# Landmark sums on the vector engine from transposed q and k, PE transposes into bf16 PSUM, and the landmark softmax of the next batch ahead of the first layer of this one

## The chip, the cores and the metric

The kernel runs on one core of a Trainium2 chip. The metric is the device time of one execution in microseconds, as the median over several runs; lower is better. The engines are named as in the profile: PE (TensorE), DVE (VectorE), ACT (ScalarE), POOL (GpSimd) and SP (SyncE).

## The reference

The work is a Nyström attention followed by a two-layer block with a SiLU between the layers, both in float32. There are 8 batches, 8 heads, 576 positions of head size 64, and 32 landmarks, each the mean of 18 neighbouring positions. The second part has 4608 tokens, width 512 and hidden width 2048.

```python
q_lm = q.reshape(B, H, m, S // m, D).mean(axis=3)      # m = 32
k_lm = k.reshape(B, H, m, S // m, D).mean(axis=3)
A  = sm(q, k_lm);  Bm = sm(q_lm, k_lm);  C = sm(q_lm, k)   # sm: scaled softmax
Z = Bm.T / (norm1(Bm) * norminf(Bm) + 1e-6)
for _ in range(6):
    Z = 2 * Z - Z @ Bm @ Z
x = (A @ Z @ C @ v)            # tokens x 512 over the heads
h = x @ w_in;  g = h * sigmoid(h);  out = g @ w_out
```

## The kernel before

**A planner sets the order.** The kernel adds operations (`A(name, engines with planned costs, emit, dependencies, priority, ...)`) to a plan. `Plan.run` goes through simulated time, gives each free engine the ready operation of lowest priority number, and the program is emitted in that order. Every engine then runs its own queue strictly in that order on the chip: an instruction whose data is late holds up all that stand behind it on its engine.

**One batch** (`attn(b)`, `layer1(b)`, `layer2_batch(b)`). The eight heads of a batch sit in two groups g of four heads, on 128 partitions. The steps, with the names that the rest of this document uses:

- *Loads.* q, k and v come in through POOL's queue (L377, L384), weights too (L391 to L401). For batches from 2 on, `later_loads` gates the load of batch b on the transposes of batch b-2 (the buffer `qk` has two halves) and of batch b-1.
- *Transposes of q and k* into `qT`. Batches 0 and 1 (`NPE = 2`): on PE, each block as an ordinary product with the identity `idb` into f32 PSUM (L485), then a cast to bf16 on DVE or ACT (`copy`, L342 and L344). Batches 2 to 7: by DMA transposes on SP's queue (L506), four for a batch, which wait for the loads.
- *Landmark sums.* Batches 0 and 1 on PE (L524). Batches 2 to 7 on POOL: a tree of five kinds of f32 additions (`sa`, `sb`, `lm`, L543), ten instructions for a batch, straight from the loaded `qk`. `ltr` turns the sums on PE, `lmT` is the copy of that to SBUF.
- *Landmark softmax and its inverse.* `sb` (scores of landmarks, PE, L576), `pb` (exp, ACT, L588), row sums and `bm` (DVE, L595, L597), `bbd`, the norm, and then six Newton steps, each a PE product of `st` and a DVE instruction (L647). I call the steps from L595 to L647 the chain.
- *The wide softmaxes.* `C` and `A` (PE, L709 and L666), exp on ACT (`ce` L718, `et` L675), sums and their inverse by Ln and exp (L685, L689), `etn` on DVE (L694). C's probabilities are turned into `ct`: for batches below `NCT = 3` by PE products and casts, for the others by DMA transposes on SP (L744). `cv`, `wsb`, `zt` and `m` (L757 to L807) put the small matrices together with w_in.
- *First layer:* 16 wide PE products and 2 narrow ones for a batch, each followed by a SiLU on ACT (`gm` L838, `gx` L861).
- *Second layer:* seven half-size products for each pair of 128 tokens (Strassen's scheme), with four DVE sums of `gm` into `ss` (L927) ahead of them, and sums of w_out made once (`wt` and `w_out_sb`, L447, eight DVE instructions).

**ACT's two tables.** Exp and Ln share one table, SiLU has another, and a change of table costs an ACT_TABLE_LOAD. The planner therefore binds all exp work of a batch into a group (`group=f"x{b}"`), which opens only when no first layer is open and no SiLU may stand inside (L137 to L146). `pb` belongs to the group of its own batch, so the landmark softmax of batch b+1, and the chain behind it, begin when the first layer of batch b is through.

**Idle PE slots** below 45 us of the plan are filled with products of zeros (`zer`), whose results are not used.

Of the kernel before, what the change touches and what calls it, by code (L numbers as in the profile page):

```python
# [7 lines left out]
FP = mybir.dt.float32  # L8
# [10 lines left out]
class Op:  # L19


    def __init__(self, name, engs, emit, deps=(), prio=0.0, psum=0, cls=None, table=None,
# [6 lines left out]
        self.after = ()  # L29
        self.ins = None  # L30
# [14 lines left out]
class Plan:  # L45
# [16 lines left out]
    def run(self):  # L62
# [50 lines left out]
        while n < total:  # L113
# [7 lines left out]
            while moved:  # L121
                moved = False
                for e in ("PE", "ACT", "DVE", "POOL", "SP"):
# [3 lines left out]
                    for o in cand[e]:  # L127
# [11 lines left out]
                        if e == "ACT" and o.group is not None and group[0] != o.group:  # L139
                            if group[0] is not None:  # L140
                                continue
                            if l1_open:
                                continue
                            if len(l1_at) > 2:
# [38 lines left out]
                    switch = False  # L183
                    if e == "ACT" and o.table and o.table != table[0]:
                        dur += 1.3
                        table[0] = o.table
                        switch = True
                    if o.group is not None:
                        if group[0] is None:
                            group[0], group[1] = o.group, groups[o.group]  # L190
                            pending[0] = False
                        group[1] -= 1
# [66 lines left out]
def kernel(  # L259
# [26 lines left out]
    NCT = 3  # L286
# [21 lines left out]
    s1_r = ring(smp, [128, NG, JP, Dh], FP, "sa", 1)  # L308
    s2_r = ring(smp, [128, NG, 4, Dh], FP, "sb", 1)
# [5 lines left out]
    bbd_r = ring(smp, [128, NG, 4, L], BF, "bbd", 1)  # L315
    st_r = ring(smp, [128, NG, SW], BF, "st", 3)
# [34 lines left out]
    def either(n, act=True, dve=True):  # L351
# [5 lines left out]
        return r  # L357

# [93 lines left out]
    bones = hmask.rearrange("p a l -> p (a l)")  # L452


    last = {}
    tree = [None]
# [4 lines left out]
    def attn(b):  # L461
# [12 lines left out]
        if on_pe:  # L474
            blocks = {}
            me["qk_read"] = []
            for t in (1, 0):
                todo = [(g, jp) for g in range(NG) for jp in range(JP)]
                for i in range(0, 18, 4):
                    part = todo[i:i + 4]  # L480
# [11 lines left out]
                    def tcp(e, t=t, i=i, n=len(part), key=(t, i)):  # L492
                        copy(e, qT[:, t].rearrange("p g j x -> p (g j) x")[:, i:i + n, :],
                             bank(blocks[key])[:, 0:n * 128].rearrange("p (n x) -> p n x", x=128))
                    c = A(f"trc{t}{i}.{b}", either(128 * len(part)), tcp, [o], p0 + 8).reads(o)
# [22 lines left out]
        for t in (1, 0):  # L518
            if on_pe:
                for j0 in range(0, J, 6):  # L520
                    def lms(e, t=t, j0=j0):
                        ps = bank(me["lms", t])
                        for j in range(j0, j0 + 6):
                            mm(ps[:, 0:128], idb, qk[:, t, :, j, :], start=(j == 0),  # L524
                               stop=(j == J - 1))
                    o = A(f"lms{t}{j0}.{b}", [("PE", mm_us(128, 6))], lms,
# [551 lines left out]
```

## Time and profile before

| what | value |
|---|---|
| runs shown (3) | 275.11, 275.89, 276.56 us; median 275.89 us |
| the profiled execution | 276.69 us, of which the span from first to last instruction is 275.0 us |
| mean granted TensorE clock | 0.973 |
| busy: PE / ACT / DVE / POOL | 254.0 / 188.6 / 171.1 / 116.7 us |
| table loads on ACT | 13 x 1.283 us |
| moved by DMA | 37.29 MB |

The profile lists for each engine how long it was busy, for each group of like instructions their count, summed and mean duration and the idle time before them, and for an idle stretch the instruction whose end released it. The zero products count as PE busy. PEclk is the clock granted to PE in a stretch, 1.00 for full speed; a busy PE at a lower clock does less.

### The profile page before, as it was taken

The page shows a single profiled execution, that of the slowest core. Times are in us where ns is not written, and L with a number is a line of the kernel's source. Part 1 is how long each engine was busy: PE and PEld are TensorE (multiplying, and loading weights), DVE is VectorE, ACT ScalarE, POOL GpSimd, SP SyncE. Part 2 cuts the span into 40 slices and gives each one's busy share as a digit, 9 for nine tenths or more (in the row PEclk, how much of TensorE's full clock was granted, in tenths as well). Part 3 has the DMA queues.
Part 4 walks back from the last instruction along what each step waited for, and adds up shares of the span by engine and source line. Part 5 has one row for each costly group of instructions (what it writes and reads, how often), then busy time and mean ns, then how long its engine had stood idle before and what let it go on. Part 6 is the DMA issues. An engine that isn't in the chain of part 4 may idle for free.

```text
span 275.0 us, 7164 instructions
## 1 busy us (share of the span) xinstructions
PE 254.0 (92%) x2773; PEld 173.0 (63%) x2773; DVE 171.1 (62%) x381; ACT 188.6 (69%) x449; POOL 116.7 (42%) x133
## 2 busy tenths in 40 slices
PE   7999999859979979789997999999999999999993
PEld 5975545633657645446565556768777657588882
DVE  1477329964197784899389749616898739154621
ACT  1699997508976689857997875586756897852120
POOL 8337513997954964992598259700000000000000
PEclk9999999977979999979999999999999999999999
DMA  6999999999999899939975999913428300202433
GB/s 101 213 195 203 206 204 210 202 146 219 181 114 158 176 165 184 184 60 186 192 130 96 183 211 191 177 38 79 76 70 129 79 0 4 75 21 72 116 78 101
DMA packets 58593, 37.29 MB, mean 136 GB/s; under 512 B 39616, under 2 KB 49856, under 8 KB 58560
## 3 DMA queue, kind: packets, MB, share of 16 engines
q0 software_dynamic: 15232, 18.35, 40.3%
q1 hardware_dynamic: 43184, 18.30, 34.1%
q8 instruction: 21, 0.34, 0.5%
q10 hardware_dynamic: 144, 0.20, 0.2%
q14 instruction: 12, 0.10, 0.1%
HBM read 36.70 MB, written 9.44 MB: 168 GB/s over the span
## 4 chain that ended last, share of the span: by engine, by line
PE 63%; DVE 16%; DMA 8%; ACT 5%; issue 4%; POOL 2%; DVEq 0%; POOLq 0%; ACTq 0%
PE ps L332 63%; DMA w_in_sb<-in_moe_w_in_dram 8%; DVE ss L927 5%; ACT gm L838 3%; DVE m L344 3%; DVE gm L927 1%; DVE wt L447 1%; POOL qk L377 1%; DVE st L647 1%; DVE bm L597 1%; DVE ost L961 1%; DVE w_out_sb L447 1%; POOL v L384 1%; ACT m L342 1%; DVE etn L694 1%
## 5 line engine op out<-in xcount | busy, mean ns | idle before, releaser
L332 PE MATMUL ps<-etn,m 128*128 128x64 bf16 (+1 forms) x512 | 71.3, 289 | 0.2 <-DVE m L344 0.2
L838 ACT ACTIVATE gm<-ps 128x512 f16<-128x512 f32 x128 | 66.0, 635 | 3.1 <-PE ps L332 2.8
L332 PEld LDWEIGHTS <-gm 128*128 128x128 f16 x512 | 48.7, 99 | 15.1 <-issue 5.4
L332 PE MATMUL ps<-w_out_sb,gm 128*128 128x256 f16 (+1 forms) x392 | 54.7, 284 | 0.6 <-DVE w_out_sb L447 0.5
L342 ACT COPY ost<-ps 128x256 f32<-128x256 f32 (+1 forms) x59 | 21.9, 375 | 48.6 <-PE ps L332 47.2
L332 PEld LDWEIGHTS <-m 128*128 128x128 bf16 x512 | 32.3, 98 | 25.4 <-issue 3.3
L332 PEld LDWEIGHTS <-ss 128*128 128x128 f16 x408 | 38.8, 98 | 9.4 <-DVE ss L927 2.4
L543 POOL TENSOR_TENSOR sa<-qk 128x576 f32<-128x576 bf16 x24 | 33.0, 1394 | 15.4 <-DMA qk<-in_k_dram 14.9
L961 DVE TENSOR_TENSOR ost<-ost,ps 128x256 f32<-128x256 f32 x51 | 20.9, 416 | 28.7 <-PE ps L332 19.7
L332 PE MATMUL ps<-wt,ss 128*128 128x256 f16 x272 | 35.1, 277 | 1.2 <-DVE ss L927 1.2
L647 DVE SCALAR_TENSOR_TENSOR st<-st,ps 128x320 bf16<-128x320 bf16 (+3 forms) x54 | 21.5, 405 | 13.1 <-PE ps L332 12.6
L543 POOL TENSOR_TENSOR sb<-sa 128x512 f32<-128x512 f32 (+1 forms) x24 | 25.1, 1044 | 1.8
L344 DVE CAST m<-ps 128x512 bf16<-128x512 f32 x31 | 20.2, 682 | 3.5 <-PE ps L332 3.4
L342 ACT CAST m<-ps 128x512 bf16<-128x512 f32 x33 | 18.0, 589 | 4.7 <-PE ps L332 4.7
L927 DVE TENSOR_TENSOR ss<-gm 128x1024 f16<-128x1024 f16 x15 | 14.8, 999 | 8.5 <-ACT gm L838 8.5
L384 POOL DMA_DIRECT2D v<-in_v_dram x24 | 14.0, 591 | 11.4 <-DMA w_out_sb<-in_moe_w_out_dram 6.1
L332 PE MATMUL ps<-w_out_sb,ss 128*128 128x256 f16 x136 | 17.7, 273 | 0.5 <-DVE ss L927 0.4
L332 PE MATMUL ps<-st 128*128 128x160 bf16 (+1 forms) x96 | 14.7, 226 | 3.7 <-DVE st L647 2.8
L718 ACT ACTIVATE ce<-ps 128x288 bf16<-128x288 f32 x32 | 12.7, 410 | 6.4 <-PE ps L332 6.4
L332 PE MATMUL ps<-wt,gm 128*128 128x256 f16 x120 | 16.4, 282 | 0.4 <-DVE ost L961 0.4
L332 PE MATMUL ps<-w_in_sb,zt 64*32 64x512 bf16 x256 | 13.6, 412 | 3.2 <-DVE m L344 2.1
L344 DVE COPY ost<-ps 128x256 f32<-128x256 f32 (+1 forms) x11 | 4.9, 449 | 18.4 <-PE ps L332 17.7
(85 smaller groups left out, 367.2 us busy)
## 6 DMA issues: line engine op xcount, KB each, us to landing
out_dram<-ost SPq DMA_DIRECT2D x141, 64.0 KB, 1.7
qk<-in_k_dram POOLq DMA_DIRECT2D x8, 576.0 KB, 6.0
qk<-in_q_dram POOLq DMA_DIRECT2D x8, 576.0 KB, 8.7
v<-in_v_dram POOLq DMA_DIRECT2D x24, 192.0 KB, 10.3
w_out_sb<-in_moe_w_out_dram POOLq DMA_DIRECT2D x4, 512.0 KB, 10.5
w_in_sb<-in_moe_w_in_dram POOLq DMA_DIRECT2D x4, 256.0 KB, 9.2
w_in_sb<-in_moe_w_in_dram POOLq DMA_DIRECT2D x8, 128.0 KB, 7.0
qT<-qk SPq DMA_TRANSPOSE x24, 3.9
```

What stands on the lines that cost most here:

```text
L332: nc.tensor.matmul(out=out_ap, lhsT=lhsT, rhs=rhs, start=start, stop=stop, skip_group_check=True)
L342: nc.scalar.copy(out=out, in_=in_)
L344: nc.vector.tensor_copy(out=out, in_=in_)
L377: lambda e, t=t, src=src: nc.gpsimd.dma_start(out=qk_r[b % 2][:, t].rearrange("p g j d -> p g (j d)"), in_=src[b].rearrange("(g h) (l j) d ...
L384: lambda e, a=a: nc.gpsimd.dma_start(out=v_r[b % 2][a * L:(a + 1) * L, :, :], in_=v[b].rearrange("h (l a x) d -> a l h (x d)", l=L, a=VA)[ ...
L447: lambda e, o_=o_, x=x, y=y: nc.vector.tensor_tensor(out=o_, in0=x, in1=y, op=OP.subtract), dep, 400.0)
L543: lambda e: nc.gpsimd.tensor_tensor(out=o_, in0=a_, in1=b_, op=OP.add),
L647: nc.vector.scalar_tensor_tensor(out=s2[:, g0:g1, lo:SW], in0=s[:, g0:g1, lo:SW], scalar=2.0, in1=ps[:, 0:NG * SW].rearrange("p (g x) -> p ...
L718: nc.scalar.activation(out=ce[:, :, 0:VP].rearrange("p (i c) (a l) -> p c a i l", c=2, a=VA)[:, c], in_=bank(me[f"C{g}"], c)[:, 0:HS].rear ...
L838: lambda e, dc=dc, cell=cell: nc.scalar.activation(out=gm[:, dc, :], in_=bank(cell["o"]), func=AF.Silu),
L927: lambda e, o_=o_[:, k], x=x[:, k], y=y[:, k], op=op: nc.vector.tensor_tensor(out=o_, in0=x, in1=y, op=op), dep, 850.0 + prio / 100)
L961: nc.vector.tensor_tensor(out=out_, in0=x, in1=y, op=OP.add)
```

## The change

Five things change.

1. **Landmark sums of batches 2 to 7** move from POOL to DVE. They are made from the transposed `qT`, in f16, in four instructions for each of q and k (names `lra` to `lrd`, 1024, 512, 256 and 256 elements per partition; tiles `red` and `rs`). The ten POOL additions of a batch go. `ltr` becomes one PE product with a constant `fold` (f16), which also adds the last two halves.
2. **PE transposes** (q and k of batches 0 and 1, and `ct`) use the transpose instruction and write bf16 into PSUM. The copies of q and k are four for each of q and k instead of five, those of `ct` one for a group of heads instead of two. `NCT` goes from 3 to 4, so batch 3's `ct` goes over PE and no longer over SP.
3. **The landmark softmax of batch n+1** may now run while the exp table of batch n is still loaded: `sb` no longer waits for what the rest of its batch needs (`ready`), `pb` is marked `early`, and `A` and `C` carry `ready` and open the group instead. The SiLUs of batch 0 wait for `pb` of batch 1.
4. **Buffers:** `st` from 3 to 6 tiles and `bbd` from 1 to 2, so that two batches' chains may overlap.
5. **The order in which operations are added:** `attn(b)` before `layer1(b - 1)`.

How the planner's order moves is seen at two places. The first is ACT's queue around the first layer of batch 0. Before, from the last SiLU of batch 0 on (`gx`; `pb1` is the landmark softmax of batch 1, `ce` belongs to its wide softmax):

```order
L861 ACTIVATE gx_120<-ps4_74 128x8x64
L1036 ACT_TABLE_LOAD
L588 ACTIVATE pb1_93<-ps5_75 128x64
L718 ACTIVATE ce0_108,pbs1_95<-ps0_70 128x3x3x32
L718 ACTIVATE ce0_108,pbs1_95<-ps1_71 128x3x3x32
```

With the change, at the beginning of the same first layer (L358 is the copy, L620 `pb`, L874 the SiLU):

```order
L358 CAST m0_120<-ps6_76 128x512
L358 CAST lmT1_91<-ps5_75 128x256
L358 CAST m0_120<-ps0_70 128x512
L620 ACTIVATE pb1_93<-ps2_72 128x64
L874 ACT_TABLE_LOAD
L874 ACTIVATE gm0_122<-ps4_74 128x512
L358 CAST m0_120<-ps5_75 128x512
```

`pb1` has moved from behind the 18 SiLUs of batch 0 to ahead of them, and the table load of the SiLUs stands behind it.

The second place is DVE's queue behind the first layer of batch 0. Before (`wt` and `w_out_sb` are the sums of w_out, `st` the Newton steps of batch 1, `etn` and `wsb` its wide softmax):

```order
L447 TENSOR_TENSOR wt_121<-w_out_sb_79,wt_121 128x1024
L647 SCALAR_TENSOR_TENSOR st1_100<-st0_99,ps0_70 128x320
L447 TENSOR_TENSOR wt_121<-w_out_sb_79,wt_121 128x1024 x2
L647 SCALAR_TENSOR_TENSOR st2_101<-st1_100,ps0_70 128x320
L694 TENSOR_TENSOR etn1_107<-et0_102,ln0_104 128x576
L774 TENSOR_TENSOR wsb1_113<-ps4_74,pbs1_95 128x256
L694 TENSOR_TENSOR etn1_107<-et1_103,ln1_105 128x576
L647 SCALAR_TENSOR_TENSOR st0_99<-st2_101,ps0_70 128x320
L447 TENSOR_TENSOR wt_121<-w_out_sb_79,wt_121 128x1024
L447 TENSOR_TENSOR w_out_sb_79<-w_out_sb_79 128x4x256
```

With the change, the Newton steps of batch 1 (L680) stand in the first layer of batch 0:

```order
L662 TENSOR_TENSOR st3_103<-ps4_74,pbs1_95 128x2x128
L680 SCALAR_TENSOR_TENSOR st4_104<-st3_103,ps0_70 128x320
L680 SCALAR_TENSOR_TENSOR st5_105<-st4_104,ps0_70 128x320
L680 SCALAR_TENSOR_TENSOR st3_103<-st5_105,ps0_70 128x320
L468 TENSOR_TENSOR wt_125<-w_out_sb_79 128x1024
L680 SCALAR_TENSOR_TENSOR st4_104<-st3_103,ps0_70 128x320
L964 TENSOR_TENSOR ss0_126<-gm0_122 128x1024
```

and where the first layer of batch 1 begins (`m1` is its input), the landmark sums of batch 2 follow (L570, `red`):

```order
L360 CAST m1_121<-ps1_71 128x512
L468 TENSOR_TENSOR wt_125<-w_out_sb_79,wt_125 128x1024 x2
L468 TENSOR_TENSOR w_out_sb_79<-w_out_sb_79 128x4x256 x2
L570 TENSOR_TENSOR red_86<-qT0_82 128x1024
L998 TENSOR_TENSOR ost2_130<-ost2_130,ps5_75 128x256
L570 TENSOR_TENSOR red_86<-red_86 128x2x256
L998 TENSOR_TENSOR ost2_130<-ost2_130,ps6_76 128x256
```

The sums of w_out no longer stand between the Newton steps of batch 1, and DVE's queue now holds additions that wait for SP's transposes (`qT`), with outputs of the second layer (`ost`) behind them.

The diff, cut to its core:

```diff
@@ Plan.run
                         if e == "ACT" and o.group is not None and group[0] != o.group:
-                            if group[0] is not None:
+                            if o.early is not None and table[0] == "exp":
+                                pass
+                            elif group[0] is not None or l1_open:
                                 continue
-                            if l1_open:
+                            elif o.early is not None and any(
+                                    x.done is None or x.done > t + 1e-9 for x in o.early):
                                 continue
+                        if o.opens is not None and group[0] != o.opens and (
+                                group[0] is not None or l1_open or len(l1_at) > 2):
+                            if group[0] is None and not l1_open:
+                                pending[0] = True
+                            continue
...
-    NCT = 3
+    NCT = 4
-    s1_r = ring(smp, [128, NG, JP, Dh], FP, "sa", 1)
-    s2_r = ring(smp, [128, NG, 4, Dh], FP, "sb", 1)
+    red = smp.tile([128, NG, 4, 128], HF, tag="red", name="red")
+    rs = smp.tile([128, 2, NG, 128], HF, tag="rs", name="rs")
-    bbd_r = ring(smp, [128, NG, 4, L], BF, "bbd", 1)
-    st_r = ring(smp, [128, NG, SW], BF, "st", 3)
+    bbd_r = ring(smp, [128, NG, 4, L], BF, "bbd", 2)
+    st_r = ring(smp, [128, NG, SW], BF, "st", 6)
+    STEPS = (((0, 5), (5, 4), (9, 5), (14, 4)),) * 2
...
+    fold = constp.tile([128, 128], HF, tag="fold", name="fold")
+    def folds(e):
+        for r in (0, 64):
+            for c in (0, 64):
+                nc.vector.tensor_copy(out=fold[r:r + 64, c:c + 64], in_=idb[r:r + 64, r:r + 64])
...
-                        ps = bank(blocks[key])
+                        ps = bank(blocks[key]).bitcast(BF)
                         for n, (g, jp) in enumerate(part):
-                            mm(ps[:, n * 128:(n + 1) * 128],
-                               qk[:, t, g, 2 * jp:2 * jp + 2, :].rearrange("p j d -> p (j d)"),
-                               idb)
+                            nc.tensor.transpose(
+                                out=ps[:, n * 128:(n + 1) * 128],
+                                in_=qk[:, t, g, 2 * jp:2 * jp + 2, :].rearrange("p j d -> p (j d)"),
+                                identity=idb)
...
-                xs = [pool(f"la{g}", 576, s1[:, g], src[:, g, 0:9], src[:, g, 9:18],
-                           [qk_ops[b, t], tree[0]]) for g in range(NG)]
-                me["qk_read"] += xs
-                x = pool("lb", 512, s2, s1[:, :, 0:4], s1[:, :, 4:8], xs)
-                x = pool("lc", 256, s1[:, :, 0:2], s2[:, :, 0:2], s2[:, :, 2:4], [x])
-                x = pool("ld", 128, s2[:, :, 0], s1[:, :, 0], s1[:, :, 1], [x])
-                tree[0] = lm_ops[t] = pool("le", 256, lm[:, t], bc(s2[:, :, 0], 2, 2),
-                                           bc(s1[:, :, 8], 2, 2), [x] + prev2.get("ltrs", []))
+                src = qT[:, t]
+                x = lr("ra", 1024, red[:, :, 0:4], src[:, :, 0:4], src[:, :, 4:8],
+                       qt_ops[t, 0] + qt_ops[t, 1] + tree[0])
+                x = lr("rb", 512, red[:, :, 0:2], red[:, :, 0:2], red[:, :, 2:4], [x])
+                x = lr("rc", 256, red[:, :, 0], red[:, :, 0], red[:, :, 1], [x])
+                x = lr("rd", 256, rs[:, t], red[:, :, 0], src[:, :, 8], [x] + prev.get("ltrs", []))
...
+                if not on_pe:
+                    return mm(ps[:, 0:256], fold, rs[:, t].rearrange("p g x -> p (g x)"))
...
-        me["sb"] = A(f"sb.{b}", [("PE", 0.2)], sbm, lmT_all + ready, p0 + 11, psum=1,
+        me["sb"] = A(f"sb.{b}", [("PE", 0.2)], sbm, lmT_all + prev2.get("zt", []), p0 + 11, psum=1,
+        pb_op.early = ready
...
-                            lmT_all + [(pb_op, -0.2)] + qt_ops[1, g], p0 + 18 + g,
+                            lmT_all + [(pb_op, -0.2)] + qt_ops[1, g] + ready, p0 + 18 + g,
+            me[f"C{g}"].opens = grp
...
-                for i0 in range(0, VI, 3):
+                for i0 in (0,):
+                        for n in range(VI):
+                            nc.tensor.transpose(out=ps[:, n * 128:(n + 1) * 128],
+                                                in_=ce[:, i0 + n, :], identity=idb)
...
-                               [o], p, table="silu").reads(o))
+                               [o] + ([last[1]["pb"]] if not b else []), p,
+                               table="silu").reads(o))
...
-    for b in range(B):
-        attn(b)
-        layer1(b)
-        layer2_batch(b)
+    for b in range(B + 1):
+        if b < B:
+            attn(b)
+        if b:
+            layer1(b - 1)
+            layer2_batch(b - 1)
```

More of the change, by code (lines that the diff above doesn't have):

```diff
@@ L29, in __init__ @@
         self.after = ()
+        self.early = None
+        self.opens = None
         self.ins = None
@@ L183, in run @@
                     switch = False
+                    switchless = table[0] == "exp"
                     if e == "ACT" and o.table and o.table != table[0]:
@@ L357, in either, with half16 @@
         return r
+    def half16(n):
+        return [("DVE", 0.07 + 0.00055 * n), ("ACT", act_us(n))]
+    STEPS = (((0, 5), (5, 4), (9, 5), (14, 4)),) * 2
     swdge = []
@@ L584, in attn @@
         bm, bmt = bm_r[b % 2][:, 0], bm_r[b % 2][:, 1]
-        bbd = bbd_r[0]
-        grp = f"x{b}"
+        bbd = bbd_r[b % 2]
+        sr = st_r[3 * (b % 2):3 * (b % 2) + 3]
+        grp = "x0" if MERGE and b < 2 else f"x{b}"
         pb_op = me["pb"] = o = A(f"pb.{b}", [("ACT", act_us(64))],
```

74 lines of the change are left out of this document (41 added, 33 removed).

## The prediction

> **What bounds the kernel now.** I read the busy time by stretches first, cut at the places where the landmark scores `sb` of batches 2 and 3 run on PE (69 and 89 us). The columns are: stretch, its length, then busy time of PE, PEld, DVE, ACT and POOL, the granted clock, DMA share and GB/s.
>
> ```profile
> 0.00:28.00 28.00, 24.96 (x345) 19.32 (x346) 14.83 (x49) 18.63 (x48) 15.89 (x29) 1.00 1.05 178
> 28.00:45.00 17.00, 17.00 (x153) 8.79 (x152) 7.21 (x18) 15.32 (x34) 4.86 (x8) 1.00 1.23 208
> 45.00:69.00 24.00, 19.95 (x189) 11.30 (x187) 17.39 (x29) 13.29 (x31) 20.74 (x20) 0.86 1.04 191
> 69.00:89.00 20.00, 18.49 (x211) 13.02 (x204) 12.64 (x29) 16.23 (x41) 12.36 (x16) 0.91 0.96 149
> 89.00:170.00 81.00, 73.16 (x828) 44.52 (x826) 62.30 (x133) 64.09 (x150) 56.04 (x58) 0.98 0.92 164
> 170.00:270.00 100.00, 99.98 (x1063) 75.92 (x1061) 56.70 (x126) 60.68 (x147) 6.85 (x6) 1.00 0.36 74
> ```
>
> PE is the bound: from 170 us on it has no gap. What can be won lies between 45 and 170 us, in two forms. PE is idle 24.00-19.95 = 4.05, 20.00-18.49 = 1.51 and 81.00-73.16 = 7.84, together 13.4 us. And it is busy at a reduced clock: 0.14 x 19.95 = 2.8, 0.09 x 18.49 = 1.7, 0.02 x 73.16 = 1.5, together 6.0 us. So the ceiling of any reordering is 19.4 us. Before 45 us PE also runs the zero products, but there the loads of the weights set the pace (below).
>
> Next, what ended PE's idle time from 45 to 170 us (sum, times, longest):
>
> ```profile
> PE ps L332 <- DVE st L647: 3.3, 4, 1.5
> PE ps L332 <- DVE m L344: 2.8, 7, 1.3
> PE ps L332 <- DVE bm L597: 1.8, 2, 1.4
> PE ps L332 <- DVE ss L927: 1.6, 2, 1.2
> PE ps L332 <- DVE st L629: 1.0, 2, 0.6
> PE ps L332 <- DVE w_out_sb L447: 0.5, 1, 0.5
> ```
>
> DVE ends 11.0 of the 13.4 us in these six rows. Of that 3.3+1.8+1.0 = 6.1 us is the chain of the landmark softmax and 2.8+1.6+0.5 = 4.9 us is DVE late with other work. How the chain is held up, in order of time (start, length, engine):
>
> ```profile
> 54.46 1.76 DVE L447 TENSOR_TENSOR w_out_sb<-w_out_sb 128x1024 f16<-128x1024 f16 x1
> 56.14 0.47 DVE L647 SCALAR_TENSOR_TENSOR st<-st,ps 128x320 bf16<-128x320 bf16 x1
> 56.67 0.31 PE L332 MATMUL ps<-st 128*128 128x160 bf16 x2 [1.46 <-DVE st L647]
> ```
>
> PE waits 1.46 us for a Newton step that stood behind a sum of w_out, and that sum took 1.76 us. The DVE groups between 45 and 178 us, while POOL makes its sums, against those after 178 us (summed us, mean ns) show why it took so long; first 45 to 178 us:
>
> ```profile
> L927 DVE TENSOR_TENSOR ss<-gm 128x1024 f16<-128x1024 f16 x7 | 9.4, 1364 | 2.2 <-ACT gm L838 2.2
> L694 DVE TENSOR_TENSOR etn<-et,ln 128x576 bf16<-128x576 bf16 x10 | 7.5, 763 | 0.8 <-ACT ln L689 0.8
> L927 DVE TENSOR_TENSOR ss<-ss,gm 128x1024 f16<-128x1024 f16 x7 | 6.8, 969 | 0.0
> L927 DVE TENSOR_TENSOR gm<-gm 128x1024 f16<-128x1024 f16 x7 | 6.3, 905 | 0.0
> L927 DVE TENSOR_TENSOR ss<-gm,ss 128x1024 f16<-128x1024 f16 x7 | 6.3, 899 | 0.0
> L447 DVE TENSOR_TENSOR wt<-w_out_sb,wt 128x1024 f16<-128x1024 f16 x4 | 5.2, 1329 | 0.0
> L447 DVE TENSOR_TENSOR w_out_sb<-w_out_sb 128x1024 f16<-128x1024 f16 x2 | 3.1, 1557 | 0.0
> L597 DVE TENSOR_TENSOR bm<-pb,pbs 128x64 bf16<-128x64 f32 x4 | 2.6, 652 | 0.1
> L603 DVE TENSOR_TENSOR bbd<-bm,hmask 128x256 bf16<-128x256 bf16 x4 | 2.2, 555 | 0.1
> ```
>
> and after 178 us:
>
> ```profile
> L927 DVE TENSOR_TENSOR ss<-gm 128x1024 f16<-128x1024 f16 x7 | 4.8, 679 | 0.0
> L603 DVE TENSOR_TENSOR bbd<-bm,hmask 128x256 bf16<-128x256 bf16 x2 | 0.6, 280 | 0.0
> L597 DVE TENSOR_TENSOR bm<-pb,pbs 128x64 bf16<-128x64 f32 x2 | 0.4, 224 | 0.1
> ```
>
> The same instruction takes 679 ns when POOL is quiet and up to 1557 ns when POOL adds: the two disturb each other.
>
> **The change part by part.** *POOL's sums go.* DVE gets back what they cost it. At 0.68 us for 1024 f16 elements the excess is 7 x (1.364+0.969+0.905+0.899 - 4 x 0.68) = 9.9, 4 x (1.329-0.68) = 2.6, 2 x (1.557-0.68) = 1.8, 4 x (0.652-0.224) = 1.7 and 4 x (0.555-0.280) = 1.1 us: 17 us.
>
> *DVE's sums come.* From 0.679 us for 1024 and 0.280 us for 256 elements (0.52 ns an element), 512 take 0.41 us, and one tensor 0.679+0.41+0.280+0.280 = 1.65 us; 12 of them (6 batches, q and k) make 19.8 us. The trace has no addition with bf16 inputs and an f16 result. The other bound is the rate of `etn`, whose one input is f32: 763 ns for 576 elements, 1.32 ns each, which makes 1.36+0.68+0.34+0.34 = 2.7 us for a tensor and 32.6 us in all. I take 19.8: `bbd` and `ss` are the nearest rows, 16-bit throughout. The Trainium skill ("VectorE: DVE Perf Modes", section "What auto-detection actually checks") says that two results per cycle are had when every tensor is 16-bit with unit step, whatever the kind; by that rule the sum is 19.8 too, and no row here shows the mixed kinds.
>
> So DVE's load stays, 19.8-17 = +3 us; below zero it can't come out on these bounds. What changes is that no single instruction holds the queue for 1.4 to 1.8 us.
>
> *The chain moves ahead of the first layer.* Its 6.1 us of PE waits go: the cover is the first layer, 16 wide products and two narrow ones, for which the chain isn't needed. If that cover failed the 6.1 us come back. Of the other 4.9 us I take half, 2.5 (ends 0 and 4.9), since the queue's longest instructions halve while the sums take their place in it. Idle time won: 8.6 us, leaving 4.8.
>
> *The clock.* It fell to 0.86 and 0.91 in the stretches with the long waits, but stood at 0.98 from 89 to 170 us, where PE was idle 7.84 of 81 us in short pieces. With 4.8 us left in 125 us the idle share is less than half of that, and so I take 0.01 of 111.6 us busy as the rest: 6.0-1.1 = 4.9 us won (ends 2, if one long wait stays in each stretch, and 6).
>
> *The SiLUs of batch 0 now wait for `pb` of batch 1.* The rows around their start:
>
> ```profile
> 27.52 0.41 PE L332 MATMUL ps<-w_in_sb,zt 64*32 64x512 bf16 x7 [0.53 <-DMA w_in_sb<-in_moe_w_in_dram]
> 28.90 1.28 ACT L838 ACT_TABLE_LOAD   x1
> 30.19 0.60 ACT L838 ACTIVATE gm<-ps 128x512 f16<-128x512 f32 x1
> ```
>
> PE stands at 27.52 us for w_in. In the new order the scores `sb` of batch 1 follow that product at about 28.3 us, `pb` ends near 28.8, and the table load stands where it stood, at 28.9. Cost 0, covered by the load of w_in; at most 0.5. The same load covers the cheaper copies of q and k (20 casts become 16): gain 0.
>
> *Transposes for `ct` of batch 3* go to PE, 12 more. The nearest row is the present transposes:
>
> ```profile
> L332 PE MATMUL ps<-qk,idb 128*128 128x128 bf16 x72 | 5.4, 219 | 1.3 <-DMA qk<-in_k_dram 0.8 <-DMA qk<-in_q_dram 0.5
> ```
>
> 5.4/72 x 12 = 0.9 us on the path. That row also carries the one rule that speaks against the change. The clock was 1.00 from 0 to 45 us with ordinary products as transposes. The Trainium skill ("TensorE: Matmul & The Clock Gate", section "Part 4: PE-mode transpose") says that transposes in PE's own mode don't count as busy for the clock gate, so the full clock isn't engaged by them. No run here shows that yet; it is a rival below.
>
> *DVE now waits for the transposes on SP.* POOL summed from the loads, DVE sums from `qT`, which comes later. The rows: issue of batches 2's and 3's transposes, the load of batch 3 between, and the times on PE of `sb` of batches 2 and 3.
>
> ```profile
> 51.59 5.63 SPq L506 DMA_TRANSPOSE qT<-qk  x4
> 59.77 0.73 POOL L377 DMA_DIRECT2D qk<-in_k_dram  x1
> 71.15 6.66 SPq L506 DMA_TRANSPOSE qT<-qk  x4
> DMA to landing us min/median/max: 3.3/3.9/5.4
> 68.88 0.22 PE L332 MATMUL ps<-lmT 64*32 64x32 bf16 x8
> 89.30 0.22 PE L332 MATMUL ps<-lmT 64*32 64x32 bf16 x8
> ```
>
> Batch 2's last transpose lands at 51.59+5.63+3.9 = 61.1 us; with 1.65 us of sums and an estimated 1 us for `ltr`, `lmT` and `sb`, the scores run at 63.8. Without any stall PE would be there at 68.88-4.05-2.8 = 62.0 plus some 2 us of work that the new order puts ahead: 64. No loss. Batch 3's load waits for the third of these transposes, at about 59.7, where it stands now, so its transposes stay at 71.15 and the scores can run at 71.15+6.66+3.9+2.65 = 84.4. PE without stalls is at 89.30-5.56-4.5 = 79.2, plus some 3 us of work put ahead (products of batch 2's `m`, `zt` and two of the second layer's): 82. Loss 2 us (bounds 0 and 5). Behind the waiting additions on DVE stand outputs `ost` of the second layer, whose PSUM banks the next products need. For later batches loads and transposes cycle in 71.15-51.59 = 19.6 us, PE in 25 or more, so their transposes come in time.
>
> *Sum:* 8.6+4.9-0.9-2 = 10.6 us. The profiled execution took 276.69 us, so 266.1; the median of the runs is 0.8 us below that execution: **265.3**.
>
> **The rivals.**
> A, *full recovery*: all waits on DVE go (11.0) and the clock holds (6.0), the transposes are in time: 275.9-17+0.9 = 259.8. For it: long DVE instructions caused the waits for `m` and `ss` too. Against it: DVE's load doesn't fall.
> B, *the clock gate and the transposes*: the clock halves in the transposes of batches 0 and 1 and w_in no longer covers it. Bounds: 0, and half of the work from 7 to 28 us, 10 us; as an estimate 4 us, so 270. Against it: zero products stand between.
> C, *no change*: POOL isn't the cause of the slow rows (they'd be slow by the loads that run up to 178 us too), DVE has 20 us more in a stretch where it is 92 of 125 us busy, and takes back the 10.6: 276.
> D, *slower*: head-of-line blocking on DVE. POOL's sums waited this long for their data without harm:
>
> ```profile
> L543 POOL TENSOR_TENSOR sa<-qk 128x576 f32<-128x576 bf16 x24 | 33.0, 1394 | 15.4 <-DMA qk<-in_k_dram 14.9
> ```
>
> If DVE waits these 14.9 us instead, for data that come later still, its queue stops everything: 265.3+14.9 = 280. It decides when DVE reaches the first addition before the second transpose of its batch has landed, for batch 2 before 51.59+1.4+3.9 = 56.9 us, in most batches. Against it: the cycle of 19.6 us.
>
> **How the numbers follow.** My forecast with its own range of 261 to 269 gets 0.53, A 0.19, B 0.08, C 0.09, D 0.11. About 0.5% (1.4 us) is what a measurement of this kernel can tell from no change. Faster by more: 0.53+0.19+0.08 = 0.80; the same 0.09; slower 0.11. The range runs from 257.5, A with the zero products of the first 45 us partly gone as well, to 272, past B and past the forecast with the longer wait for transposes (3 us more) and the lower end of the clock term (2.9 us less); it leaves out C and D.
>
> **What would show it.** Right: DVE's f16 sums at 0.68 us throughout; no PE wait ended by `st` or `bm` between 45 and 170 us; PE idle there near 5 to 7 us; `sb` of batch 3 near 84 us. Wrong: a clock below 1.00 before 28 us (B); DVE idle in front of the landmark sums, released by DMA, with PE idle beside it (D); the additions at over 1 us each (C); a first SiLU later than 31 us.

## The result and the profile after

The changed kernel takes 259.65 us (median of 4 runs, 258.67 to 262.15) where the kernel before takes 275.73 us beside it: a ratio of 0.943 [0.935, 0.951]. The forecast was 265.3 us in a range of 257.5 to 272; the gain is 16.1 us where the sum said 10.6. Rival A, full recovery, had 259.8.

The profiled execution is the longest of the four, 262.15 us with a span of 260.4. Its busy time by the stretches of the prediction (the same columns: PE, PEld, DVE, ACT, POOL, granted clock, DMA share, GB/s):

```profile
0.00:28.00 28.00, 25.10 (x338) 18.78 (x338) 14.32 (x55) 17.99 (x42) 16.00 (x29) 1.00 1.05 179
28.00:45.00 17.00, 17.00 (x172) 8.96 (x170) 10.39 (x27) 16.39 (x37) 4.74 (x8) 1.00 1.23 207
45.00:69.00 24.00, 23.11 (x249) 13.83 (x248) 17.13 (x37) 20.46 (x47) 3.13 (x5) 1.00 1.06 186
69.00:89.00 20.00, 17.19 (x214) 12.61 (x208) 15.59 (x45) 10.85 (x31) 3.13 (x5) 1.00 0.96 174
89.00:170.00 81.00, 79.46 (x856) 50.19 (x855) 55.18 (x138) 72.21 (x174) 9.43 (x15) 1.00 0.93 168
```

PE's idle time between 45 and 170 us is 0.89 + 2.81 + 1.54 = 5.2 us, where it was 13.4, and the clock stands at 1.00 in every stretch. The most is won where most was lost, from 45 to 69 us (4.05 to 0.89) and from 89 us on (7.84 to 1.54); the middle stretch has more idle time than before, 2.81 against 1.51. What ended the idle time from 45 to 170 us (sum, times, longest):

```profile
PE ps L348 <- ACT ost L358: 1.4, 2, 1.2
PE ps L348 <- DVE st L680: 1.1, 3, 0.7
PE ps L348 <- DVE ost L998: 0.8, 3, 0.3
PE ps L348 <- DVE rs L570: 0.5, 1, 0.5
PE ps L348 <- ACT lmT L358: 0.4, 1, 0.4
```

The waits for `bm`, `m` and w_out are gone, and of the chain 1.1 us is left of 6.1. The longest wait is a new one, for `ost`: two output copies on ACT wait 3.0 us for a free output buffer, whose stores stand behind a batch's transposes on SP's queue.

The DVE groups from 45 to 178 us (summed us, mean ns); the first four are the landmark sums, the others answer to the groups that were slow beside POOL's additions:

```profile
L570 DVE TENSOR_TENSOR red<-qT 128x1024 f16<-128x1024 bf16 x12 | 8.3, 691 | 7.4 <-DMA qT<-qk 7.4
L570 DVE TENSOR_TENSOR red<-red 128x512 f16<-128x512 f16 x12 | 5.0, 420 | 0.1
L570 DVE TENSOR_TENSOR red<-red 128x256 f16<-128x256 f16 x12 | 3.4, 285 | 0.1
L570 DVE TENSOR_TENSOR rs<-red,qT 128x256 f16<-128x256 f16 x12 | 3.5, 288 | 0.2
L964 DVE TENSOR_TENSOR ss<-gm 128x1024 f16<-128x1024 f16 x8 | 5.4, 684 | 1.6 <-ACT gm L874 1.6
L468 DVE TENSOR_TENSOR wt<-w_out_sb,wt 128x1024 f16<-128x1024 f16 x4 | 2.6, 683 | 0.0
L468 DVE TENSOR_TENSOR w_out_sb<-w_out_sb 128x1024 f16<-128x1024 f16 x2 | 1.3, 686 | 0.0
L630 DVE TENSOR_TENSOR bm<-pb,pbs 128x64 bf16<-128x64 f32 x5 | 1.1, 219 | 0.0
```

`ss` is at 684 ns where it was at 1364, `w_out_sb` at 686 where it was at 1557, `bm` at 219 where it was at 652. The sums took 8.3 + 5.0 + 3.4 + 3.5 = 20.2 us, and DVE waited 7.4 us for the transposes. Over the whole span DVE is busy 164.1 us where it was 171.1.

The places of batches 2 and 3 (start, length): transposes on SP, and the scores `sb` on PE.

```profile
51.06 6.66 SPq L536 DMA_TRANSPOSE qT<-qk  x4
63.32 0.22 PE L348 MATMUL ps<-lmT 64*32 64x32 bf16 x8
71.90 5.60 SPq L536 DMA_TRANSPOSE qT<-qk  x4
83.99 0.23 PE L348 MATMUL ps<-lmT 64*32 64x32 bf16 x8
```

`sb` of batch 2 runs at 63.32 us where it stood at 68.88, that of batch 3 at 83.99 where it stood at 89.30.

### The profile page after: what moved, and what is told of

Same layout as the page of the kernel before. It is cut to its first block, busy times and chain, and to the rows that moved or that the text cites. A ratio compares the mean times of both kernels' runs of the same rounds, so it can differ in the third digit from the quotient of the medians.

```text
span 260.4 us, 7063 instructions
## 1 busy us (share of the span) xinstructions
PE 247.4 (95%) x2760; PEld 169.4 (65%) x2760; DVE 164.1 (63%) x420; ACT 189.2 (73%) x454; POOL 36.4 (14%) x61
## 4 chain that ended last, share of the span: by engine, by line
PE 66%; DMA 15%; ACT 7%; SPq 4%; DVE 3%; issue 2%; POOL 1%; ACTq 0%; DVEq 0%; POOLq 0%
PE ps L348 65%; DMA out_dram<-ost 5%; DMA qk<-in_q_dram 5%; DMA qT<-qk 4%; SPq L536 2%; ACT gm L874 2%; SPq L941 2%; ACT L874 1%; ACT m L358 1%; POOL qk L398 1%; DVE red L570 1%; ACT ost L358 1%; PE ps L768 1%; ACT ce L753 1%; ACT ct L358 1%
## 5 line engine op out<-in xcount | busy, mean ns | idle before, releaser
L874 ACT ACTIVATE gm<-ps 128x512 f16<-128x512 f32 x128 | 66.8, 661 | 1.3 <-PE ps L348 1.1
L358 ACT COPY ost<-ps 128x256 f32<-128x256 f32 (+1 forms) x62 | 23.2, 380 | 47.2 <-PE ps L348 42.2
L348 PE MATMUL ps<-w_out_sb,gm 128*128 128x256 f16 (+1 forms) x392 | 53.7, 282 | 0.3 <-DVE ost L998 0.2
L680 DVE SCALAR_TENSOR_TENSOR st<-st,ps 128x320 bf16<-128x320 bf16 (+3 forms) x54 | 21.5, 406 | 10.5 <-PE ps L348 9.7
L360 DVE CAST m<-ps 128x512 bf16<-128x512 f32 x29 | 19.3, 687 | 5.6 <-PE ps L348 4.8
L358 ACT CAST m<-ps 128x512 bf16<-128x512 f32 x35 | 19.6, 598 | 3.3 <-PE ps L348 3.2
L398 POOL DMA_DIRECT2D qk<-in_k_dram x8 | 5.8, 729 | 94.5 <-DMA qT<-qk 55.8
L348 PE MATMUL ps<-wt,gm 128*128 128x256 f16 x120 | 15.6, 273 | 0.2 <-DVE ost L998 0.2
L728 DVE TENSOR_TENSOR etn<-et,ln 128x576 bf16<-128x576 bf16 x16 | 12.1, 755 | 4.0 <-ACT ln L723 3.8
L348 PEld LDWEIGHTS <-st 128*128 128x128 bf16 x96 | 8.3, 97 | 9.1 <-DVE st L680 1.8
L709 ACT ACTIVATE et<-ps 128x288 bf16<-128x288 f32 x32 | 11.5, 425 | 2.6 <-PE ps L348 2.6
L570 DVE TENSOR_TENSOR red<-qT 128x1024 f16<-128x1024 bf16 x12 | 8.3, 691 | 7.4 <-DMA qT<-qk 7.4
```

Source lines behind the costliest of these rows:

```text
L348: nc.tensor.matmul(out=out_ap, lhsT=lhsT, rhs=rhs, start=start, stop=stop, skip_group_check=True)
L358: nc.scalar.copy(out=out, in_=in_)
L360: nc.vector.tensor_copy(out=out, in_=in_)
L398: lambda e, t=t, src=src: nc.gpsimd.dma_start(out=qk_r[b % 2][:, t].rearrange("p g j d -> p g (j d)"), in_=src[b].rearrange("(g h) (l j) d ...
L570: lambda e: nc.vector.tensor_tensor(out=o_, in0=a_, in1=b_, op=OP.add),
L680: nc.vector.scalar_tensor_tensor(out=s2[:, g0:g1, lo:SW], in0=s[:, g0:g1, lo:SW], scalar=2.0, in1=ps[:, 0:NG * SW].rearrange("p (g x) -> p ...
```

## The experiments

Three readings stood against each other. The forecast's own: the chain ahead of the first layer and the sums on DVE are separate gains that add up. Its rivals: one of the two makes nearly all of the gain; or the two need each other, and neither gains alone. Beside them stood the question what the waits and transfers cost that the change brings in. Since the planner forms the whole order anew when anything in the plan changes, the first four runs change the order too; the four after them keep the order of every queue but for the edit; the last four measure what a new order alone does.

**The sums back on POOL, the chain still ahead.**

```diff
-                src = qT[:, t]
-                x = lr("ra", 1024, red[:, :, 0:4], ...
+                src = qk[:, t]
+                xs = [pool(f"la{g}", 576, s1[:, g], src[:, g, 0:9], ...
...
-                if not on_pe:
-                    return mm(ps[:, 0:256], fold, ...)
```

> The changed kernel (259.65 us) with one part undone: the landmark sums of batches 2 to 7 are again POOL's ten additions from qk, and ltr is two products. The landmark softmax ahead, the transposes and NCT = 4 stay. Theory 1 (most of the gain is the chain moved ahead of the first layer; the sums' move is worth the 2.5 us of DVE lateness that I took, less the waits for transposes): 261 to 264 us, DVE's 1024-element additions again at 0.9 to 1.4 us between 45 and 165 us, granted clock 0.99 or more. Rival 2 (the slow DVE instructions were the main cause, the order of the chain a detail): 269 us or more, with PE waits ended by DVE's st and m back at over 8 us.

275.77 us, ratio 0.999 [0.995, 1.004]: nothing is left of the gain. The time is on the side of the expectation's rival, but its waits are not: `st` and `m` end 2.0 us of PE's idle time from 45 to 170 us, where it asked for over 8. From 45 to 70 us this kernel is as good as the change (PE busy 24.30 of 25 us at clock 1.00, the change 23.90), so the chain ahead does clear that stretch; it loses from 70 us on. The timeline there shows the two ways in which POOL's sums hurt (start, length, in brackets the idle time before and what ended it):

```profile
106.78 0.29 PE L348 MATMUL ps<-idb,lm 128*128 128x128 bf16 x2 [1.97 <-POOL lm L566]
...
113.37 2.27 DVE L722 TENSOR_TENSOR etn<-et,ln 128x576 bf16<-128x576 bf16 x1
115.57 0.15 DVE L623 RECIPROCAL pbs<-pbs 128x2 f32<-128x2 f32 x1
115.65 0.16 DVE L360 CAST zt<-ps 128x32 bf16<-128x32 f32 x1
115.76 0.56 DVE L624 TENSOR_TENSOR bm<-pb,pbs 128x64 bf16<-128x64 f32 x1
116.36 0.19 PE L348 MATMUL ps<-bm,hmask 128*128 128x64 bf16 x1 [1.83 <-DVE bm L624]
```

PE stands for POOL's last addition, 1.97 us; and `etn` of 0.76 us takes 2.27 beside POOL's additions, and PE waits 1.83 us for `bm`, which stands behind it.

**The sums on DVE, the chain not ahead.**

```diff
-        me["sb"] = A(f"sb.{b}", [("PE", 0.2)], sbm, lmT_all + prev2.get("zt", []), ...
-        pb_op.early = ready
+        me["sb"] = A(f"sb.{b}", [("PE", 0.2)], sbm, lmT_all + ready, ...
...
-    for b in range(B + 1):
-        if b < B:
-            attn(b)
-        if b:
-            layer1(b - 1)
-            layer2_batch(b - 1)
+    for b in range(B):
+        attn(b)
+        layer1(b)
+        layer2_batch(b)
```

> The changed kernel with the other part undone: the landmark softmax of a batch again belongs to its own exp group behind the first layer of the batch before, operations are added in the old order, st has 3 tiles and bbd 1. The sums stay on DVE, the transposes and NCT = 4 stay. Theory 1: the 6.1 us of chain waits and 3 to 5 us of clock come back, 268 to 271 us; granted clock below 0.985. Rival 2: 262 to 264 us, clock near 1.00, since the chain's instructions are quick again.

277.91 us, ratio 1.003 [0.999, 1.006], beyond both expected ranges. POOL is quiet here (36.5 us busy), and still nothing is gained. Rival D of the prediction has come in, at the place that it named:

```profile
59.65 0.69 DVE L570 TENSOR_TENSOR red<-qT 128x1024 f16<-128x1024 bf16 x1 [4.67 <-DMA qT<-qk]
60.49 1.14 PE L348 MATMUL ps<-w_in_sb,zt 64*32 64x512 bf16 x15 [3.63 <-DVE zt L360]
```

DVE reaches batch 2's first addition at 59.65 - 4.67 = 54.98 us, ahead of the 56.9 us that the rival had as its point, and 4.67 us before the data are there. The copy `zt` stands behind it, and PE waits 3.63 us for `zt`; the clock from 45 to 70 us is 0.86 as before the change. It is one batch, where the rival spoke of most, and not the whole loss: PE is idle for 15.7 us between 45 and 165 us, and the SiLUs (`gm` on ACT) end another 3.0 us of that. So "the gains add up" fell, and so did "one of them makes it".

**The ordinary identity products for q and k of batches 0 and 1.**

```diff
-                for i, n in STEPS[b]:
+                for i in range(0, 18, 4):
...
-                        ps = bank(blocks[key]).bitcast(BF)
+                        ps = bank(blocks[key])
...
-                            nc.tensor.transpose(...)
+                            mm(ps[:, n * 128:(n + 1) * 128], ..., idb)
```

> The changed kernel with q and k of batches 0 and 1 transposed as before: ordinary products with the identity into f32 PSUM, five casts for each of q and k. ct stays on the new transposes. Theory 1: the load of w_in covers this, 259.0 to 260.5 us, first SiLU within 0.5 us of the changed kernel's. Rival: the cheaper bf16 copies (0.43 against 0.69 us on DVE) bring the start forward by 1 us or more, so 260.7 us or more here.

266.94 us, 7.3 us above the change, ratio to before 0.963 [0.957, 0.969]. The loss isn't where the products are: from 28 to 45 us PE is busy 16.95 us, from 45 to 70 us 24.95 (the change 17.00 and 23.90). It lies behind 70 us, in another order: the wide softmax of batch 1 goes ahead of the first SiLU here, whose table load starts at 35.81 us (28.80 in the change).

**`ct` of batch 3 back on SP, with the planner told.**

```diff
-    NCT = 4
+    NCT = 3
```

> The changed kernel with NCT = 3: ct of batch 3 goes over SP's DMA transposes again. Theory 1 (12 transposes on PE cost their 0.9 us and nothing else changes): 258.7 to 259.6 us. Rival (SP's queue, where transposes and stores stand in one line, is the next thing that holds PE): 261 us or more, with later qT transposes of the following batches.

264.85 us, ratio to before 0.957 [0.952, 0.962]: 5.2 us above the change, in a new order as well.

**The same order, the additions issued on POOL.** The four additions stay where they were in the plan, and read `qT`; only the engine is another.

```diff
-                             lambda e: nc.vector.tensor_tensor(out=o_, in0=a_, in1=b_, op=OP.add),
+                             lambda e: nc.gpsimd.tensor_tensor(out=o_, in0=a_, in1=b_, op=OP.add),
```

> The changed kernel (259.65 us) with every engine's order kept as it is, but the four additions of each landmark sum of batches 2 to 7 are issued on POOL instead of DVE, on the same f16 data from qT. Undoing the parts one at a time let the planner form another order each time, so this keeps the order. Theory 3 (the two parts need each other: the landmark softmax can only run ahead if the sums are there soon after the data, and DVE makes them in 1.7 us where POOL's tree took 6 to 8): the scores of batches 2 and 3 come 4 to 8 us later and PE waits for them, 268 to 276 us. Theory 1 (the sums' place hardly matters): 260 to 263 us.

285.10 us as the median of four runs, 283.82 without the longest, which is the profiled one (287.61); ratio to before 1.028 [1.019, 1.037]. That is 24 to 25 us above the change, slower than before it, and beyond the 268 to 276 us that were expected. The POOL group of the first addition, and PE's two waits in batch 2:

```profile
L570 POOL TENSOR_TENSOR red<-qT 128x1024 f16<-128x1024 bf16 x12 | 26.3, 2193 | 71.4 <-DMA qT<-qk 64.7 <-ACT pb L620 6.4
```

```profile
63.42 0.27 PE L348 MATMUL ps<-rs,fold 128*128 128x256 f16 x1 [3.71 <-POOL rs L570]
69.81 0.37 PE L348 MATMUL ps<-rs,fold 128*128 128x256 f16 x1 [3.21 <-POOL rs L570]
```

What takes DVE 0.69 us takes POOL 2.19. PE waits 10.7 us for `rs` between 45 and 165 us, and 3.5 for `ss`, which is disturbed again: the `gm` sums on DVE take 1109 ns in place of 684. With the chain ahead, the sums' latency stands on PE's path. Loads stand between these additions in POOL's queue (batch 3's q at 61.18 us, in the change at 59.62); what that costs is not separated.

**The same order, and POOL adds for nobody.** Five f32 additions of 576 elements behind each tensor's sums, 60 in all, with inputs and outputs of their own, so no instruction of the kernel waits for one.

```diff
+            if getattr(o, "noise", False):
+                for _ in range(5):
+                    nc.gpsimd.tensor_tensor(out=nzo, in0=nz, in1=nz, op=OP.add)
```

> The changed kernel, order kept, with five more f32 additions of 576 elements on POOL behind each landmark sum (60 in all, as many as POOL had before), on scratch tiles for which nobody waits. What they can do is disturb DVE, and hold the loads behind them in POOL's queue for some us. Theory 1's part on the disturbance: DVE's 1024-element additions at 0.8 to 1.4 us beside POOL's, 8 to 17 us more DVE time, of which a quarter to a third reaches PE: 262 to 266 us. Rival (DVE has slack enough in this order): below 260.7 us.

296.63 us, ratio to before 1.073 [1.068, 1.079]: 37 us above the change, and some 30 us beyond the expected 262 to 266. DVE is busy 202.0 us where the change has 164.1. POOL's group, and batch 2's q sums on DVE beside it (in the change 0.69 and 0.42 us):

```profile
L1085 POOL TENSOR_TENSOR nzo<-nz 128x576 f32<-128x576 f32 x60 | 79.0, 1317 | 4.2
```

```profile
60.48 2.14 DVE L573 TENSOR_TENSOR red<-qT 128x1024 f16<-128x1024 bf16 x1 [0.73 <-DMA qT<-qk]
62.66 1.25 DVE L573 TENSOR_TENSOR red<-red 128x512 f16<-128x512 f16 x1
```

So 79.0 us of POOL additions cost DVE 37.9 us of busy time, 0.48 us for each microsecond of them. That the kernel's time grows by about as much is not shown to be more than chance: the waits of PE for DVE between 45 and 200 us come to 24.3 us, and the clock is lower too (0.85 to 0.93 from 45 to 165 us). The loads are no explanation for the first part of this: those of q and k start at 59.46 and 80.25 us, 0.5 and 1.6 us later than in the change. The loads of v stand behind the additions, at 67.30 where they stood at 60.33, and what that costs is not separated.

**The same order, and no wait for the transposes.** The additions read the half of `qT` that holds the batch before, which is there in time. The landmarks are then those of another batch, so this kernel leaves out a part of the computation.

```diff
-                src = qT[:, t]
+                src = qT_r[(b - 1) % 2][:, t]
```

> The changed kernel, order kept, but the landmark sums read the other half of qT, that of the batch before, so that DVE's 7.4 us of waiting for the DMA transposes go (the landmarks of batches 2 to 7 are then those of another batch). My sum charged 2 us for these waits. Theory 1: 257.5 to 259 us, scores of batch 3 a few us earlier. Rival: no change within 0.7 us, because A and C wait for the same transposes anyway and the queue behind the sums isn't urgent.

258.95 us, ratio to before 0.938 [0.932, 0.945], against 0.943 [0.935, 0.951] for the change. The medians differ by 0.7 us, the intervals overlap, and 258.95 lies in both expected ranges, so the times don't decide what the 7.4 us of DVE's waits cost. In the profiled executions (the change's is its longest) PE is idle for 5.1 us from 45 to 155 us with the waits and for 2.4 us without. Most of that lies between 70 and 105 us, first the change, then this kernel:

```profile
70.00:105.00 35.00, 32.00 (x369) 22.39 (x369) 25.53 (x70) 25.48 (x62) 4.54 (x7) 1.00 0.92 175
70.00:105.00 35.00, 33.95 (x406) 24.08 (x404) 27.07 (x75) 27.99 (x70) 4.55 (x7) 1.00 1.02 193
```

So the waits may cost nothing, or some 3 us. Without them DVE starts batch 3's sums at 77.21 us, no earlier than the change's 76.77: DVE had other work.

**The same order, `ct` of batch 3 by DMA transposes on SP.**

```diff
+                        if b == 3:
+                            return None
                         ps = bank(me["ctm", g, i0]).bitcast(BF)
...
+                        nc.sync.dma_start_transpose(out=ct, in_=ce.rearrange("p i x -> p (i x)")),
```

> The changed kernel, order kept, with ct of batch 3 made by two DMA transposes on SP instead of 12 PE transposes and two copies. Theory 1 (0.9 us of PE work saved, nothing else): 258.5 to 259.5 us. Rival (the transposes on SP take 2.5 us to issue and 2.8 us to land, behind stores in the same queue, and cv of batch 3 stands in PE's queue): 261 to 265 us, with one PE wait of 2 us or more released by the DMA of ct.

267.73 us, ratio to before 0.967 [0.960, 0.973]: 8.1 us above the change, and 2.7 us beyond the rival's range. The two transposes land 9.1 and 10.0 us after their issue, where the expectation had 2.8. One wait makes nearly all of it (PE's waits from 70 to 165 us):

```profile
PE ps L348 <- DMA ct<-ce: 6.9, 1, 6.9
```

and it moves the queue of SP behind it:

```profile
101.79 5.08 SPq L779 DMA_TRANSPOSE ct<-ce  x2
119.07 6.59 SPq L536 DMA_TRANSPOSE qT<-qk  x4
```

In the change the latter stand at 111.94 us.

**Other orders of the same work.** The planner leaves a margin between the arrival of a product's inputs and the product. At 0.38 us instead of 0.40 it forms another order of the same instructions. Four kernels got that edit: the change, the kernel before, and the two halves of the change from above.

```diff
-    MARGIN = 0.4
+    MARGIN = 0.38
```

> The kernel after the change, with the planner's margin (the slack that it leaves between the arrival of a product's inputs and the product) at 0.38 us where it was 0.40: the work is the same, the planner forms another order. Theory that the two parts need each other, and that orders formed anew scatter by no more than about 3 us: 257 to 264 us. Rival, the gain of the change is in good part one lucky order: 267 us or more, up to the 275 of the kernel before.

> The kernel before the change, with the planner's margin at 0.38 us where it was 0.40. Theory that the two parts need each other, scatter of orders up to 3 us: 272 to 279 us. Rival, the order of the kernel before was an unlucky one: 269 us or less, and the change is then worth less than 16 us against an ordinary order of the same work.

> Landmark softmax ahead, sums back on POOL, with the margin at 0.38 us. With margin 0.40 it took 275.8. Theory that the two parts need each other: again 272 to 279 us. Rival, the parts add up and 275.8 was an unlucky order: the chain ahead alone is worth about half the change, 264 to 270 us.

> Sums on DVE, the landmark softmax not ahead, with the margin at 0.38 us. With margin 0.40 it took 277.9. Theory that the two parts need each other: again 273 to 281 us. Rival, the parts add up and 277.9 was an unlucky order: the sums on DVE alone are worth about half the change, 264 to 270 us.

Medians in us, with the ratio to the kernel before for the new column:

| kernel | margin 0.40 | margin 0.38 | ratio at 0.38 |
|---|---|---|---|
| before | 275.73 to 276.51 | 277.06 | 0.999 [0.995, 1.003] |
| chain ahead, sums on POOL | 275.77 | 279.85 | 1.010 [1.006, 1.014] |
| sums on DVE, chain not ahead | 277.91 | 278.28 | 1.006 [1.002, 1.010] |
| the change | 259.65 | 264.48 | 0.953 [0.947, 0.959] |

The picture is the same in both columns: each half alone gains nothing, both together gain 16.1 and 12.6 us. A new order alone moves the time by up to 4.8 us, half a microsecond beyond what was expected for the change and 0.9 us beyond for the first half. The half without the chain ahead repeats its wait, in the other order:

```profile
59.00 0.69 DVE L570 TENSOR_TENSOR red<-qT 128x1024 f16<-128x1024 bf16 x1 [4.34 <-DMA qT<-qk]
59.84 0.95 PE L348 MATMUL ps<-w_in_sb,zt 64*32 64x512 bf16 x15 [3.29 <-DVE zt L360]
```

In the change at margin 0.38 one place shows what an order can cost:

```profile
98.45 0.69 DVE L570 TENSOR_TENSOR red<-qT 128x1024 f16<-128x1024 bf16 x1 [3.34 <-DMA qT<-qk]
99.18 0.42 DVE L570 TENSOR_TENSOR red<-red 128x512 f16<-128x512 f16 x1
99.52 0.48 DVE L680 SCALAR_TENSOR_TENSOR st<-st,ps 128x320 bf16<-128x320 bf16 x1
...
100.06 0.44 PE L348 MATMUL ps<-qT,lmT 64*32 64x288 bf16 x8 [2.45 <-DVE st L680]
```

and its stretches around it (PE busy, granted clock, DMA share, GB/s):

```profile
95.00:100.00 5.00, 2.60 (x32) 0.98 1.06 199
100.00:105.00 5.00, 4.71 (x56) 0.68 0.78 130
```

The same addition that waits 0.50 us in the change, behind a Newton step, stands here ahead of one. It waits 3.34 us, the step waits behind it, PE for the step, and the clock falls to 0.68 after the gap. That is rival D once more, in small. It doesn't explain the 4.8 us: the two profiled executions of the change are only 1.7 us apart (spans of 260.4 and 262.1 us), and at margin 0.38 PE is less idle elsewhere.

The losses of the third and fourth run, 7.3 and 5.2 us, are not far from these 4.8 us, so they say nothing sure of the transposes or of the planner's `NCT`; the run with `ct` of batch 3 on SP in the kept order does. Not tried: the first 28 us with the zero products as transposes too, which would have put rival B to the test by itself. No run that does the whole computation was faster than the change.

## Why the prediction was right in sign and short in size

The mechanism was right in its parts: PE idles less between 45 and 170 us, DVE's long instructions were POOL's doing, the chain's waits go, the clock comes back. The sum fell short by 4.0 us on the profiled execution (262.15 for 266.1), and the median lies in the stated range but below the forecast's own 261 to 269. Its terms against the trace:

| term | forecast | in the profiled execution |
|---|---|---|
| idle time from 45 to 170 us, less the waits for transposes | 8.6 - 2 = 6.6 won | 13.4 - 5.2 = 8.2 won |
| clock | 4.9 won | 6.0 won, none left |
| `ct` of batch 3 on PE | 0.9 lost | 0.1 lost (36 in 3.6 us became 48 in 3.7) |
| zero products before 45 us | 0 | 1.4 won (12.4 us became 11.0) |

That is 15.5 us where the sum had 10.6; the span fell by 14.6, and the other 0.9 us lies in small groups, among them the landmark sums of batches 0 and 1 on PE (`ps<-qk,idb`, 5.4 us became 6.0). The prediction took that row for the transposes of q and k. Those are the row in which `qk` is the loaded weight, before and after:

```profile
L332 PE MATMUL ps<-idb,qk 128*128 128x128 bf16 x72 | 5.5, 219 | 0.0
L513 PE MATMUL ps<-idb,qk 128*128 128x128 bf16 x72 | 5.5, 218 | 0.1
```

The price for 12 of them, 0.9 us, comes out the same. The other 1.7 us of the miss is the step from the profiled execution to the median: 0.8 us before, 2.5 after.

*The waits for qT:* the times were right (`sb` forecast at 63.8 and 84.4, run at 63.32 and 83.99). Whether the price of 2 us was, stays open: the run without the waits allows nothing as well as 3 us. PE's idle time in the stretch from 69 to 89 us was ended by `ost` and `st` in pieces of at most 1.2 us, none of it by the sums themselves. So which part of the idle time was mis-sized, by 1.6 us in all, is not shown.

*`ct` of batch 3* was booked as a price of 0.9 us with nothing gained for it, as if the way over SP were free. Before the change PE had no wait for it. In the change's order the way over SP costs 8.1 us, so this part, too, can't be priced alone.

*DVE's load* was forecast to rise by 3 us, and not to fall on the bounds given. It fell by 7.0 (171.1 to 164.1). The sum left out that `st` (L621, 408 to 221 ns) and `gx` were slow beside POOL as well, 2.2 us, and that copies became fewer or cheaper (`qT`, `lmT`, `ost`, `m`, `zt`), some 6 us. The argument against rival A, that DVE's load doesn't fall, rested on this.

*Rival A* had 259.8, the figure nearest to the median, and that is in part luck. The clock came back whole, as it said, but the idle time fell by 8.2 us where it had 11.0. For the profiled execution it comes to 276.69 - 17 + 0.9 = 260.6, which took 262.15; the rest of the likeness is the step to the median, 2.5 us in place of 0.8.

*The clock* was given a rest of 1.1 us by the idle share. It went to 1.00 with 5.2 us of idle time left. So the term was 1.1 us too small. What brings the clock down the runs don't settle. It was 0.68 behind a gap of 2.45 us and 0.86 over a stretch with one of 3.63; but before the change it was also 0.86 from 45 to 69 us with no wait above 1.46, and with the sums back on POOL it held 1.00 from 45 to 165 us with waits of 1.97 and 1.83.

*The additions* took 20.2 us for 19.8 forecast. The Trainium skill's rule ("VectorE: DVE Perf Modes", section "What auto-detection actually checks") was followed by the trace: bf16 inputs with an f16 result take 691 ns for 1024 elements, all-f16 ones 684.

*POOL's disturbance:* 17 us were to come back to DVE. Of the groups named, `ss`, `gm`, `wt`, `w_out_sb`, `bm` and `bbd` fell by 8.9 + 1.5 + 2.6 + 1.8 + 1.7 + 1.1 = 17.6 us. That POOL caused them, and not the loads, is shown by the additions for nobody: they bring slow rows back (`ss` at 808 to 936 ns, `gm` at 846, `bbd` at 376). Rival C is out.

*Start of the SiLUs:* forecast unchanged, 28.9 for the table load. It starts at 28.80.

*Rival B:* the clock is 1.00 from 0 to 45 us, and a transpose takes 218 ns where the ordinary product took 219. By the rule of the Trainium skill ("TensorE: Matmul & The Clock Gate", section "Part 4: PE-mode transpose") such transposes don't engage the full clock. This trace shows no fall, but it doesn't test the rule: zero products and ordinary products stand between, and no more than 18 transposes, 1.29 us, run in a row.

*Rival D* was real, but small here: it shows in both orders of the kernel without the chain ahead, and in one place of the change's other order. In the order that the change got, DVE waits for a transpose nine times between 45 and 170 us, 1.7 us at most, and PE waits 0.5 us for the sums.

*What the prediction's reasoning lacked* is that its terms were added as if each stood alone. The chain's 6.1 us and POOL's 17 us were taken for separate causes. The runs show that taking away either leaves the time where it was: with the chain ahead but sums on POOL, PE waits for the sums and for a disturbed chain (1.97 and 1.83 us); with the sums on DVE but the chain behind the first layer, DVE's queue stops in front of `zt` (3.63 us). Together they are worth 16.6 to 18 us more than the two single effects added up (259.65 against 275.8 + 277.9 - 276.0 = 277.7; 264.48 against 279.85 + 278.28 - 277.06 = 281.1). Why the gap is as large as that is only partly shown: the waits named are some of it, and the rest lies in orders that differ throughout. One corner is also missing: the halves kept the new transposes and `ct` of batch 3 on PE, and no run has these without either half. The kernel before stands for it in the sums above, which is exact only if they are worth nothing by themselves.

## What to carry to other kernels

Price a move of work between engines by the chain that it feeds, not by the engine's load: here the same additions on POOL cost 24 to 25 us in the same order; PE waited 10.7 us for their results and 3.5 for sums on DVE that they slowed. Where a planner forms the order, undo one part in the kept order as well, and time one or two other orders of the same work before an effect of a few microseconds is believed. Look at what stands behind a waiting instruction: 7.4 us of waits in short pieces moved the median by 0.7 us, within its interval, while behind one of 4.67 us PE stood for 3.63.

## What was not expected of the hardware

The disturbance was expected, its size was not: additions on POOL that touch no data of the kernel slowed DVE by 0.48 us for each microsecond that they ran, and one instruction to three times its length (0.69 to 2.14 us). A copy of 128x512 bf16 from PSUM on DVE takes 421 ns where the f32 one took 690; on ACT the two hardly differ (592 and 597 ns).
